# The last 20 destinations of a sampled-graph aggregation as one row of their own

## The chip, the core and the metric

The kernel runs on one core of one Trainium2 chip. The metric is the device time of one execution in microseconds (us). The engines are TensorE (PE for its matmuls, PEld for its weight loads), VectorE (DVE), ScalarE (ACT), GpSimd (POOL) and SyncE (SP); SP, ACT and POOL also issue DMA transfers.

## The reference

There are 12,500 nodes with 64 features and 800,000 edges with random source and destination. For each destination the features of its sources are summed, the sum is scaled by a given factor for each node, and two 64x64 products are added:

```python
N, deg, D = 12500, 64, 64
E = N * deg
nsum = _segment_sum(x[src], dst, N)
h_neigh = nsum * deg_inv[:, None]
return x @ w_self + h_neigh @ w_neigh
```

A destination has about 64 edges, so the last 20 destinations have about 1,280 of them.

## The kernel before, in words

**Buckets.** Destinations stand in 79 blocks of 160 (two halves of `HN` = 80), sources in `NB` = 98 blocks of 128. An edge belongs to the bucket (destination block, source block); there are `NBID` = 79 x 98 = 7742 buckets with about 104 edges each. The 79th block has only 20 destinations, since 12,500 = 78 x 160 + 20, so its 98 buckets hold about 13 edges each. An edge is one 32-bit key: destination block, source block, half, source within the block, destination within the half.

**Sorting.** `sort_edges` lays the 800,000 keys out as 128 runs of 6,250 and sorts each run on DVE. `find_rows` counts in every run how many keys lie below the first key of each of 256 rows. A row is a stretch of consecutive buckets: the first part has 128 rows of 37 buckets, the second 128 rows of 24 (`KPRS`). POOL gathers each row's piece out of each run (`gather_runs`), and DVE merges the 128 pieces of every row (`merge_runs`, L446).

**Finding buckets.** `find_and_gather` handles one bucket number k of all 128 rows at a time. `count_below` (L592 for the second part, on DVE) counts the keys below the middle of bucket k in a window of the merged row. The window must hold that place for each of the 128 rows, so the planning class `Windows` makes it as wide as the spread between the rows (5.5 standard deviations at either end). Four steps later (`LAG`) ACT turns the count into an address (L615) and POOL gathers 190 keys around it (L596). `decode_buckets` splits the keys: DVE (L633 to L638), ACT casts (L643, L647), POOL writes the sources to memory (L645), PE transposes (L653), ACT stores the destinations in `dlT` (L654). Keys outside the 64 slots of a half-bucket go through `leftovers`, and `rest` gathers their feature rows in groups of 128 (L811) and adds them with a matmul (L827).

**Summing.** `nodes` walks the buckets in tiles of 8. `one_hots` prepares 28 buckets at a time: SP loads their sources, copied to all partitions (L761), DVE compares them with the partition number (L763) and the destinations with a ramp (L766). For each bucket PE multiplies the 128 feature rows by the first one-hot (`ct`, L792), ACT or DVE copies a tile of eight out of PSUM (`xg`, L802 or L800; DVE takes part from tile 503 on), and two more matmuls add the bucket into the accumulators of its destinations (`acc`, L847). Six destination blocks make a group. At its end the accumulators are copied to `g` (L851 on ACT, L853 on DVE), and `finish` multiplies 480 destinations at a time by the weights (L911), scales them, adds the self term (L917, L918) and stores them (L919). The self terms are loaded by `load_own` (L895).

**Order.** From the sort on, every engine executes its instructions in the order in which this Python code issues them. The loop over `nodes` in `sums_and_merge` interleaves the rest: while tiles of the first part are summed, the second part is merged, then found (one step each second tile), then decoded (one step a tile), then its leftovers are handled. An engine that waits holds all that stands behind it in its queue. `finish` uses SP for its store where the self terms were loaded ahead, and POOL elsewhere.

The kernel also counts every key that it has placed; if the sum is not 800,000, a slow general path (`general`) computes the result instead.

Of the kernel before, what the change touches and what calls it, by code (L numbers as in the profile page):

```python
# [11 lines left out]
F32 = mybir.dt.float32  # L12
BF = mybir.dt.bfloat16
FH = mybir.dt.float16
I32 = mybir.dt.int32
U32 = mybir.dt.uint32
# [6 lines left out]
NB = 98  # L23
H = 64
HN = 80
NDB = -(-N // (2 * HN))
NBID = NDB * NB
FB = 120
NQ = -(-N // (4 * FB))
# [1 line left out]
PITCH1 = 6400  # L31
UPPER1 = 3500

KPRS = (37, 24)
ROWS = (128, 128)
BASE = (0, 128 * KPRS[0])
NCOL = 128 * sum(KPRS)
# [28 lines left out]
LAST = 20  # L66
LAG = 4
OCT = 6


def bid_base(b):
    b = np.asarray(b)
    v = 0x40000000 | (b // NB << 22) | (b % NB << 15)
    return np.where(b >= NBID, 0x7F000000, v).astype(np.uint32)


def bid_cum(mid=False):

    size = np.minimum(128, N - 128 * np.arange(NB))
    dsize = np.minimum(2 * HN, N - 2 * HN * np.arange(NDB))  # L80
    c = np.concatenate([[0], np.cumsum(np.outer(dsize, size))]) / float(N) ** 2
    if mid:
        c[:-1] += np.outer(np.minimum(HN, dsize), size).ravel() / float(N) ** 2
    return np.concatenate([c, np.ones(NCOL - NBID)])


class Windows:
# [56 lines left out]

def constants():
    thr = bid_base(np.concatenate([BASE[p] + np.arange(ROWS[p]) * KPRS[p] for p in range(2)]))
    act = np.array([on_act(c) for c in range(NC1)])
    t1 = np.where(act, -(thr - 1).view(np.float32), thr.view(np.float32))
    mul = np.where(act, -1.0, 2.0)
    add = np.array([(n if a else 0) + lo - 1 for (lo, n), a in zip(WIN.w1, act)])  # L150
    add[128:] -= UPPER1
    assert max(lo + 2 * n for lo, n in WIN.w1[:128]) + WIDE[0] <= SPLITS[1]
    assert min(lo for lo, _ in WIN.w1[128:]) > UPPER1
    c1 = np.zeros((128, 3, NC1), np.float32)
    c1[:, 0], c1[:, 1], c1[:, 2] = t1, mul, add
    out = {"c1": c1}
    for p in range(2):
        kpr = KPRS[p]
        b = BASE[p] + np.arange(128)[:, None] * kpr + np.arange(kpr)[None]
        v = bid_base(np.minimum(b, NBID))  # L160
        act = np.array([on_act2(p) for k in range(kpr)])
        first = np.array([lo + (n / 2 + 0.25 if a else 0) for (lo, n), a in zip(WIN.w2[p], act)])
        mid = v | np.uint32(1 << 14)
        c2 = out[f"c2_{p}"] = np.zeros((128, 6, kpr), np.float32)
        c2[:, 0] = v.view(np.float32)
        c2[:, 1] = mid.view(np.float32)
        c2[:, 2] = -(mid - 1).view(np.float32)
        c2[:, 3] = np.where(act, -0.5, 1.0)
        at = [home(p, k) for k in range(kpr)]
        c2[:, 4] = first + np.arange(128)[:, None] * np.array(PITCH2)[at] - np.where(np.array(at) == 1, UPPER2 + SIDE, 0)  # L170
        c2[0::2, 5, 0] = c2[1::2, 5, 1] = 1.0
    return out
# [79 lines left out]
class Kernel:  # L252
# [10 lines left out]
    def setup(self):  # L263
# [4 lines left out]
        self.idf = keep.tile([128, 128], F32, name="idf")  # L268
        make_identity(nc, self.idf)
        self.xh = keep.tile([128, NB, 2, D], FH, name="xh")  # L270
        self.cnt = keep.tile([128, sum(NCNT) + 3], F32, name="cnt")
        nc.gpsimd.memset(self.cnt, 0.0)
        self.deg = keep.tile([FB, 4 * NQ], F32, name="deg")
        self.wn = keep.tile([128, D], F32, name="wn")
# [414 lines left out]
    def leftovers(self, part, mps):  # L689
# [42 lines left out]
        self.left[part] = (place, src)  # L732
        yield 1

    def uses(self):


        out = []
        for o in range(0, NBID, OCT * NB):
            end = min(o + OCT * NB, NBID)  # L740
            here = []
            for p in range(2):
                for c in range(64):
                    lo = max(o, BASE[p] + c * 2 * KPRS[p])
                    hi = min(end, BASE[p] + (c + 1) * 2 * KPRS[p])
                    if hi > lo:
                        here.append([hi + 56, p, c, lo // NB, (hi - 1) // NB])
            at = end + 8
            for use in sorted(here)[::-1]:
                at = use[0] = min(use[0], at - 24)  # L750
            out += sorted(here)
        return out
# [16 lines left out]
    def nodes(self, pool, aps, mps):  # L769
# [61 lines left out]
        def sums(job):  # L831
# [17 lines left out]
            if last:  # L849
# [5 lines left out]
                for q in range(2):  # L855
                    if (2 * o + q) * 4 * FB < N:
                        late.append([b0 + 40 * (1 + 3 * q), self.finish(2 * o + q, g[:, q * 4 * FB:(q + 1) * 4 * FB],
                                                                        self.fin, mps, self.w2n, own)])
            return last

        tiles = []
# [3 lines left out]
        for t, (b0, cnt) in enumerate(tiles):  # L865
# [8 lines left out]
                else:  # L874
                    late[0][0] = b0 + 40
            if t == len(tiles) - 12:
                own = self.load_own(NQ - 1, self.fin)
            done.append(t)
            yield t
        for job in pend:  # L880
# [171 lines left out]
    def sums_and_merge(self, es, mps, aps, u1, other, l2, l2b, l2a, va, vp):  # L1052
# [17 lines left out]
        va.close()  # L1070

        self.fin = fin = es.enter_context(tc.tile_pool(name="fin", bufs=1, side="right"))
        find = decode = None
        self.left = {}
        self.picked, self.used = -9, 0
        left, left_at = self.leftovers(0, mps), 2
        t = 0
        for n in self.nodes(fin, aps, mps):
# [7 lines left out]
                    left_at = n + wait  # L1086
            if runs and n % 2:
                self.gather_runs(1, u1, [runs.pop(0)])
            if merge and n >= 8 and (n >= RESUME or steps < 2 * per):
                t += PACE  # L1090
                while merge and t > 0:
# [13 lines left out]
            elif find:  # L1105
                if n % 2 == 0 and self.picked < n - 1 and next(find, None) is None:
                    find = None
                    decode = self.decode_buckets(1, self.v, vp, mps)
            elif decode:
                if next(decode, None) is None:  # L1110
                    assert n < 128 * KPRS[0] // 8 - 12
# [31 lines left out]
```

## Time and profile before

| | |
|---|---|
| time, three runs | 1947.45 us median (1946.54 to 1955.99) |
| the profiled execution, its own time | 1940.29 us |
| its span, first to last instruction | 1938.5 us |
| busy: DVE, ACT, PE, POOL | 88%, 61%, 50%, 41% of the span |
| granted clock of TensorE, mean | 0.794 of full speed |

The summing loop fills the time from about 840 us to the end; PE is mostly idle before it. The stretches that the change touches all lie in this loop: 1291 to 1384 us (finding the second part), 1384 to 1426 us (decoding it), 1426 to 1500 us (its leftovers), and the end from 1900 us.

In a row of a timeline stand the start, the duration, the engine, the line, the operation, what it writes and reads, and in brackets how long the engine was idle before it and what ended that. A row of a stretch has busy time and count for each engine, the granted clock, the DMA share and GB/s. A row of waits has who waited for whom, the total in us, how often, and the longest.

### The profile page before, as it was taken

How to read it: one execution, taken by the hardware profiler on the slowest of the kernel's cores; microseconds unless marked ns; L12 is line 12 of the kernel's file. 1: busy time of each engine (PE TensorE's matmuls, PEld its weight loads, DVE VectorE, ACT ScalarE, POOL GpSimd, SP SyncE). 2: the span in 40 equal slices, each digit the busy share in tenths (PEclk: the TensorE clock that was granted, in tenths of full speed). 3: DMA queues.
4: the chain of work that ended last, by engine and by line, in shares of the span. 5: the costliest groups of instructions: out<-in, count | busy, mean ns of one | idle time of the engine just before them, and what ended most of it. 6: DMA issues, size and time to landing. Idle time of an engine off the chain costs nothing.

```text
span 1938.5 us, 55055 instructions
## 1 busy us (share of the span) xinstructions
PE 978.3 (50%) x23940; PEld 852.7 (44%) x23940; DVE 1707.2 (88%) x1729; ACT 1177.3 (61%) x1845; POOL 789.2 (41%) x904
## 2 busy tenths in 40 slices
PE   0043000000000000158888898886879998999896
PEld 0032000000000000047777777775768787887785
DVE  7999999995749997878799999999988889888884
ACT  7363007423510023448888898887868887888785
POOL 1000000498889984888423131325422233232231
PEclk9996555555555555579999999999989999999998
DMA  4332000011110012257677877887757888888873
GB/s 149 68 75 57 0 0 28 26 52 21 22 20 10 10 44 69 55 207 258 213 240 237 259 248 252 251 291 234 247 200 263 283 285 259 275 268 262 275 249 107
DMA packets 104053, 308.61 MB, mean 159 GB/s; under 512 B 51823, under 2 KB 59359, under 8 KB 103163
## 3 DMA queue, kind: packets, MB, share of 16 engines
q1 hardware_dynamic: 85963, 280.86, 40.9%
q0 software_dynamic: 17264, 22.07, 8.6%
q8 instruction: 189, 3.10, 0.6%
q10 hardware_dynamic: 576, 2.07, 0.3%
q14 instruction: 61, 0.50, 0.1%
HBM read 285.51 MB, written 19.44 MB: 157 GB/s over the span
## 4 chain that ended last, share of the span: by engine, by line
DVE 45%; PE 22%; POOL 15%; issue 10%; DMA 4%; ACT 3%; DVEq 0%; SPq 0%; ACTq 0%; POOLq 0%
DVE u L446 14%; PE ct L792 11%; POOL u L384 11%; PE acc L847 8%; DVE ohd L766 8%; DVE a L220 7%; DVE b L220 6%; DVE ohs L763 5%; POOL pad L297 3%; DVE junk L592 1%; DMA slb<-sl 1%; DVE u L406 1%; DMA lx<-xt,lsrc 1%; ACT xg L802 1%; DMA rd<-dst 1%
## 5 line engine op out<-in xcount | busy, mean ns | idle before, releaser
L802 ACT ACTIVATE xg<-ct 128x1024 f16<-128x1024 f32 (+1 forms) x909 | 864.2, 1034 | 171.0 <-PE ct L792 147.2
L792 PE MATMUL ct<-xh,ohs 128*128 128x128 f16 x7742 | 548.8, 224 | 63.8 <-DVE ohs L763 42.2
L792 PEld LDWEIGHTS <-ohs 128*128 128x128 f16 x7742 | 456.1, 100 | 104.9 <-issue 38.0
L384 POOL DMA_INDIRECT u<-d,ix x256 | 359.0, 1402 | 232.7 <-DVE ix L376 191.0
L847 PE MATMUL acc<-ohd,xg 64*128 64x80 f16 x15484 | 407.3, 200 | 66.0 <-issue 32.5
L446 DVE TENSOR_TENSOR u<-u 128x1456 f32<-128x1456 f32 (+46 forms) x292 | 393.7, 1377 | 21.6 <-ACT u L411 14.6
L847 PEld LDWEIGHTS <-xg 64*128 64x128 f16 x15484 | 323.5, 96 | 134.3 <-issue 62.2
L766 DVE TENSOR_TENSOR ohd<-iota,dlT 128x2240 f16<-128x2240 bf16 x277 | 365.4, 1319 | 0.0
L811 POOL DMA_INDIRECT lx<-xt,lsrc x140 | 234.4, 1675 | 286.1 <-PE acc L827 250.1
L763 DVE TENSOR_SCALAR ohs<-slb,pidx 128x3584 f16<-128x3584 bf16 x277 | 319.7, 1154 | 32.6 <-PE ct L792 23.9
L374 PE MATMUL stp<-idf,st 128*128 128x128 f32 x2 | 0.9, 447 | 368.0 <-DVE st L372 368.0
L919 POOL DMA_DIRECT2D out<-o x26 | 25.1, 964 | 375.1 <-DVE o L918 285.7
L220 DVE TENSOR_TENSOR a<-b 128x764 f32<-128x764 f32 (+39 forms) x104 | 171.6, 1693 | 3.9
L220 DVE TENSOR_TENSOR b<-a 128x764 f32<-128x764 f32 (+39 forms) x104 | 171.5, 1691 | 3.6
L374 PEld LDWEIGHTS stp<-idf,st 128*128 128x128 f32 x2 | 0.4, 183 | 368.4 <-issue 368.4
L653 PE MATMUL tr<-idb,l 128*128 128x128 bf16 x61 | 8.1, 271 | 284.1 <-ACT l L647 280.6
L800 DVE CAST xg<-ct 128x1024 f16<-128x1024 f32 x66 | 80.8, 1223 | 64.1 <-PE ct L792 63.8
L653 PEld LDWEIGHTS <-l 128*128 128x128 bf16 x61 | 5.0, 116 | 287.4 <-ACT l L647 283.2
L411 ACT ACTIVATE u<-u 128x30 f32<-128x30 f32 (+34 forms) x136 | 29.7, 265 | 152.5 <-DVE u L446 77.3
L596 POOL DMA_INDIRECT v<-d,ix x61 | 80.2, 1314 | 61.5 <-ACT ix L615 30.8
L222 ACT ACTIVATE b<-a 128x1 f32<-128x1 f32 (+21 forms) x52 | 18.1, 379 | 134.5 <-DVE a L220 129.4
L590 ACT ACTIVATE junk<-u,c 128x166 bf16<-128x166 f32 (+36 forms) x37 | 26.7, 723 | 119.1 <-DVE u L446 119.0
(136 smaller groups left out, 868.3 us busy)
## 6 DMA issues: line engine op xcount, KB each, us to landing
slb<-sl SPq DMA_DIRECT2D x277, 896.0 KB
u<-d,ix POOLq DMA_INDIRECT x256
xt<-xh SPq DMA_DIRECT2D x1, 3136.0 KB
fo<-own SPq DMA_DIRECT2D x26, 120.0 KB
out<-o POOLq DMA_DIRECT2D x26, 120.0 KB
own<-os SPq DMA_DIRECT2D x12, 256.0 KB
lx<-xt,lsrc POOLq DMA_INDIRECT x140
rd<-dst SPq DMA_DIRECT2D x4, 521.0 KB
```

The lines of the kernel that those rows point to most:

```text
L220: nc.vector.tensor_tensor(view(dst, lo + sh, [[st, g], [1, l]]), x, y, op=op)
L297: self.nc.gpsimd.memset(self.pad, 0.0)
L384: nc.gpsimd.indirect_dma_start(out=u[:nr, EDGE + p * w:EDGE + (p + 1) * w], out_offset=None, in_=src, in_offset=bass.IndirectOffsetOnAxis( ...
L446: nc.vector.tensor_tensor(view(dst, EDGE + o + out, d), view(src, EDGE + o + x, d), view(src, EDGE + o + x + gap, d), op=op)
L596: self.nc.gpsimd.indirect_dma_start(out=self.v[:, k].bitcast(F32), out_offset=None, in_=flat(self.d2[home(part, k)], 128 * PITCH2[home(par ...
L763: nc.vector.tensor_scalar(s.rearrange("p c s -> p (c s)"), b, self.pidx[:, :1], None, op0=OP.is_equal)
L766: nc.vector.tensor_tensor(d, self.iota[:, None].to_broadcast([128, 14, HN, 2]), ix, op=OP.is_equal)
L792: nc.tensor.matmul(ct[:, i * 128:(i + 1) * 128], cols[i][0], self.xh[:, (b0 + i) % NB].rearrange("p a f -> p (a f)"), start=True, stop=True)
L800: nc.vector.tensor_copy(xg[:, :cnt * 128], ct[:, :cnt * 128])
L802: nc.scalar.activation(xg[:, :cnt * 128], ct[:, :cnt * 128], AF.Copy)
L811: nc.gpsimd.indirect_dma_start(out=x, out_offset=None, in_=self.xt, in_offset=bass.IndirectOffsetOnAxis(ap=self.left[p][1][:, c:c + 1], ax ...
L847: nc.tensor.matmul(acc[h][:, db % OCT * HN:(db % OCT + 1) * HN], xg[r, i * 128:(i + 1) * 128], d[r], start=db % OCT == 0 and sb == 0, stop ...
```

## The change

The last 20 destinations get no buckets. There are 78 destination blocks and 7644 buckets, and rows of the second part hold 23 buckets. The buckets now fill the first 127 rows of that part, and the threshold of the 128th row is set to the first key of the 79th block (`TAIL`), so that this row collects the keys of the last 20 destinations and nothing else. After the merge a new generator, `tail`, reads 128 x 14 keys of that row, splits them, gathers the feature row of each key (14 indirect DMAs of 128 rows), makes a 128x20 one-hot for each 128 keys, adds them with 14 matmuls, and runs `finish` for the 20 destinations. It advances by one step each second tile, from the end of finding on. The self terms of the last two sets of 480 destinations, not those of the last 20, are now loaded ahead.

```diff
-NDB = -(-N // (2 * HN))
+NDB = N // (2 * HN)
-KPRS = (37, 24)
+KPRS = (37, 23)
+LEAST = 2 * HN * NDB
+LEND = 14
+TAIL = np.uint32(0x40000000 | NDB << 22)
...
-    return np.concatenate([c, np.ones(NCOL - NBID)])
+    return np.concatenate([c, np.full(NCOL - NBID, c[-1])])
...
+    thr[-1] = TAIL
...
+    def tail(self, mps):
+        nc = self.nc
+        pool = self.fin
+        n = LEND
+        k = pool.tile([128, n], I32, name="tk")
+        last = self.d2[2][127, SIDE:SIDE + 128 * n]
+        nc.gpsimd.dma_start(k.bitcast(F32), last.rearrange("(p n) -> p n", n=n))
+        yield
+        yield
...
+        nc.vector.tensor_scalar(s, k, 8, 0x3F80, op0=OP.logical_shift_right, op1=OP.bitwise_and)
+        nc.vector.tensor_scalar(t, k, 7, 0x7F, op0=OP.logical_shift_right, op1=OP.bitwise_and)
+        nc.vector.tensor_tensor(s, s, t, op=OP.bitwise_or)
+        yield
...
+        nc.vector.tensor_scalar(t, k, 21, 0xFE, op0=OP.logical_shift_right, op1=OP.bitwise_and)
+        nc.vector.tensor_scalar(z, t, float(2 * NDB), None, op0=OP.is_equal, op1=OP.add,
+                                accum_out=self.cnt[:, sum(NCNT) + 3:sum(NCNT) + 4])
+        nc.vector.tensor_scalar(q, k, 127, None, op0=OP.bitwise_and)
+        nc.vector.scalar_tensor_tensor(q, t, float(HN), q, op0=OP.mult, op1=OP.add)
+        nc.vector.tensor_scalar(t, k, 14, 1, op0=OP.logical_shift_right, op1=OP.bitwise_and)
+        nc.vector.scalar_tensor_tensor(z, t, float(HN), q, op0=OP.mult, op1=OP.add)
+        rows = pool.tile([128, n, 128], FH, name="tx")
+        for c in range(n):
+            yield
+            nc.gpsimd.indirect_dma_start(
+                out=rows[:, c], out_offset=None, in_=self.xt,
+                in_offset=bass.IndirectOffsetOnAxis(ap=s[:, c:c + 1].bitcast(U32), axis=0))
+        m = pool.tile([128, n, N - LEAST], FH, name="tm")
+        for c in range(n):
+            if c % 4 == 0:
+                yield
+            nc.vector.tensor_scalar(m[:, c], self.wide[:, :N - LEAST], z[:, c:c + 1], -float(LEAST),
+                                    op0=OP.subtract, op1=OP.is_equal)
+        yield
+        yield
+        yield
+        ps = mps.tile([128, N - LEAST], F32, name="tps", tag="ct", bufs=3)
+        for c in range(n):
+            nc.tensor.matmul(ps, rows[:, c], m[:, c], start=c == 0, stop=c == n - 1)
+        g = pool.tile([128, N - LEAST], F32, name="tg")
+        nc.scalar.activation(g, ps, AF.Copy)
+        yield
+        for _ in self.finish(NQ - 1, g, pool, mps, self.w2n):
+            yield
+            yield
...
-                                                                        self.fin, mps, self.w2n, own)])
+                                                                        self.fin, mps, self.w2n, own and own[q])])
...
-                own = self.load_own(NQ - 1, self.fin)
+                own = [self.load_own(NQ - 3 + q, self.fin) for q in range(2)]
...
+            if tail and n % 2:
+                next(tail, None)
...
+                    tail = self.tail(mps)
```

The lines of the changed file are numbered higher: L592 there is L599, L643 and L645 are L650 and L652, L811 is L868, L919 is L976.

The first place where the order differs is DVE's queue near the end of finding (the last four windows of 24 before, the last three of 23 now). Before:

```order
L766 TENSOR_TENSOR ohd<-iota,dlT 128x2240
L819 TENSOR_SCALAR ohl<-wide,lp_2467 128x160
L853 COPY g<-acc_13573 128x6x80
L592 TENSOR_SCALAR junk_15896,acc_1_14110<-u,c_1_68 128x2229
L763 TENSOR_SCALAR ohs<-slb,pidx 128x3584
L766 TENSOR_TENSOR ohd<-iota,dlT 128x2240
L592 TENSOR_SCALAR junk_15962,acc_1_14110<-u,c_1_68 128x2329
L763 TENSOR_SCALAR ohs<-slb,pidx 128x3584
L766 TENSOR_TENSOR ohd<-iota,dlT 128x2240
L592 TENSOR_SCALAR junk_16026,acc_1_14110<-u,c_1_68 128x2428
L592 TENSOR_SCALAR junk_16091,acc_1_14110<-u,c_1_68 128x2527
```

After:

```order
L823 TENSOR_TENSOR ohd<-iota,dlT 128x2240
L876 TENSOR_SCALAR ohl<-wide,lp_2467 128x160
L910 COPY g<-acc_13573 128x6x80
L599 TENSOR_SCALAR junk_15896,acc_1_14110<-u,c_1_68 128x549
L820 TENSOR_SCALAR ohs<-slb,pidx 128x3584
L823 TENSOR_TENSOR ohd<-iota,dlT 128x2240
L599 TENSOR_SCALAR junk_15962,acc_1_14110<-u,c_1_68 128x561
L820 TENSOR_SCALAR ohs<-slb,pidx 128x3584
L823 TENSOR_TENSOR ohd<-iota,dlT 128x2240
L599 TENSOR_SCALAR junk_16026,acc_1_14110<-u,c_1_68 128x573
```

The places stay the same, but the windows shrink: from 127 to 2527 keys wide (32,579 in sum) to 114 to 573 wide (9,197 in sum). Before, a row of the second part could hold buckets of the 79th block, with an eighth of the keys of the others, and the window of bucket k had to hold both; now all buckets are alike.

The second place is POOL's queue while the second part is decoded; `tk` are the keys of the last row, `tx` their feature rows, `sl` the sources of four decoded buckets, `lx` the feature rows of leftovers. Before:

```order
L811 DMA lx<-xt,lsrc_2469 128x128 x2
L645 DMA sl<-l_16701 128x512
L919 DMA out<-o 120x4x64
L645 DMA sl<-l_16836 128x512
L645 DMA sl<-l_16968 128x512
L811 DMA lx<-xt,lsrc_2469 128x128
L645 DMA sl<-l_17102 128x512
L645 DMA sl<-l_17232 128x512
```

After:

```order
L749 DMA tk<-d_2_66 128x14
L652 DMA sl<-l_16580 128x512
L868 DMA lx<-xt,lsrc_2469 128x128
L770 DMA tx<-xt,ts 128x128
L652 DMA sl<-l_16730 128x512
L976 DMA out<-o 120x4x64
L770 DMA tx<-xt,ts 128x128 x2
L652 DMA sl<-l_16867 128x512
L770 DMA tx<-xt,ts 128x128 x2
L652 DMA sl<-l_17001 128x512
L868 DMA lx<-xt,lsrc_2469 128x128
```

Two `tx` gathers now stand ahead of most of the `sl` writes. The 14 gathers are issued over 28 tiles, and the matmuls that read them are issued seven steps (14 tiles) after the last of them.

The third place is ACT's queue at the end of the loop. Before:

```order
L851 ACTIVATE g<-acc_29310 128x6x80
L802 ACTIVATE xg<-ct 128x1024 x9
L912 ACTIVATE o<-po 120x256
L802 ACTIVATE xg<-ct 128x1024
L802 ACTIVATE xg<-ct 128x256
L851 ACTIVATE g<-acc_31537 128x80
L912 ACTIVATE o<-po 120x256
L912 ACTIVATE o<-po 20x64
```

After:

```order
L859 ACTIVATE xg<-ct 128x1024 x12
L969 ACTIVATE o<-po 120x256
L859 ACTIVATE xg<-ct 128x1024 x42
L859 ACTIVATE xg<-ct 128x512
L908 ACTIVATE g<-acc_29388 128x6x80
L969 ACTIVATE o<-po 120x256 x2
```

The 13 tiles of the 79th block and their copy to `g` are gone; the two sets of 480 destinations of the last full group, which before were finished during and after those tiles, now come after the last `g` together.

More of the change, by code (lines that the diff above doesn't have):

```diff
@@ L146, in constants @@
     thr = bid_base(np.concatenate([BASE[p] + np.arange(ROWS[p]) * KPRS[p] for p in range(2)]))
+    assert thr[-1] == 0x7F000000 and thr[-2] < TAIL
+    thr[-1] = TAIL
     act = np.array([on_act(c) for c in range(NC1)])
@@ L270, in setup @@
         self.xh = keep.tile([128, NB, 2, D], FH, name="xh")
-        self.cnt = keep.tile([128, sum(NCNT) + 3], F32, name="cnt")
+        self.cnt = keep.tile([128, sum(NCNT) + 4], F32, name="cnt")
         nc.gpsimd.memset(self.cnt, 0.0)
@@ L733, in leftovers @@
         yield 1
+    def tail(self, mps):
[7 more added lines that the diff above has]
+        yield
+        t = pool.tile([128, n], I32, name="tt")
+        s = pool.tile([128, n], I32, name="ts")
+        nc.vector.tensor_scalar(s, k, 8, 0x3F80, op0=OP.logical_shift_right, op1=OP.bitwise_and)
+        nc.vector.tensor_scalar(t, k, 7, 0x7F, op0=OP.logical_shift_right, op1=OP.bitwise_and)
+        nc.vector.tensor_tensor(s, s, t, op=OP.bitwise_or)
+        yield
+        q = pool.tile([128, n], I32, name="tq")
+        z = pool.tile([128, n], F32, name="tz")
+        nc.vector.tensor_scalar(t, k, 21, 0xFE, op0=OP.logical_shift_right, op1=OP.bitwise_and)
[29 more added lines that the diff above has]
+            yield
@@ L1072, in sums_and_merge @@
         self.fin = fin = es.enter_context(tc.tile_pool(name="fin", bufs=1, side="right"))
-        find = decode = None
+        find = decode = tail = None
         self.left = {}
```

## The prediction

> **What bounds the kernel now.** I read the span first, then the stretches of the summing loop, then the waits and the chain in the stretches that the change touches. Columns: us, then busy time and count of PE, PEld, DVE, ACT, POOL, the clock, the DMA share, GB/s.
>
> ```profile
> span 1938.5 us, 55055 instructions
> ...
> 1000.00:1291.00 291.00, 251.36 (x6401) 218.63 (x6402) 290.50 (x265) 254.01 (x291) 72.74 (x38) 0.97 0.78 251
> 1291.00:1384.00 93.00, 73.15 (x1806) 64.38 (x1807) 90.25 (x106) 73.92 (x102) 46.00 (x32) 0.90 0.76 249
> 1384.00:1426.00 42.00, 33.37 (x851) 28.48 (x850) 40.75 (x68) 41.16 (x54) 20.72 (x17) 1.00 0.78 249
> 1426.00:1500.00 74.00, 62.50 (x1538) 55.58 (x1540) 62.89 (x94) 52.02 (x59) 12.51 (x9) 0.88 0.69 230
> ...
> 1500.00:1900.00 400.00, 361.42 (x9455) 317.51 (x9449) 343.45 (x371) 322.30 (x348) 115.57 (x78) 0.99 0.84 270
> ```
>
> The bound moves. From 1000 to 1291 us (merging) DVE is busy 290.5 of 291. In finding, 1291 to 1384, DVE is busy 90.25 of 93, while PE and ACT need 73 and 74. In decoding, 1384 to 1426, ACT is full (41.16 of 42) with DVE just behind (40.75). After 1500 PE leads with 361 of 400. The share of DVE over the whole span (88%) would hide this.
>
> What a bucket costs in each stretch follows from the count of its first matmul (PE busy and count, PEld, clock, DMA):
>
> ```profile
> 1000.00:1291.00 291.00, 148.91 (x2088) 122.28 (x2088) 0.97 0.78 251
> 1291.00:1384.00 93.00, 42.59 (x588) 35.62 (x589) 0.90 0.76 249
> ...
> 1500.00:1900.00 400.00, 210.25 (x3071) 175.16 (x3072) 0.99 0.84 270
> ```
>
> That is 0.139 us a bucket in merging, 0.158 in finding, 0.130 at the end (400 / 3071). Finding is the slow one, and the waits say why; the third row is of the stretch 1426 to 1500.
>
> ```profile
> PE acc L847 <- DVE g L853: 8.2, 1, 8.2
> PE ct L792 <- DVE ohs L763: 8.0, 4, 2.7
> ...
> PE lps L727 <- DVE lab L724: 9.3, 1, 9.3
> ```
>
> In finding PE stands 19.9 us (93 - 73.15), and 16.2 of them it waits for DVE: for one-hots, and once for the copy of a finished accumulator. On DVE's timeline that copy stands behind the counts:
>
> ```profile
> 1291.01 0.34 DVE L592 TENSOR_SCALAR_CACHE_REDUCE junk<-u,c 128x127 bf16<-128x127 f32 x1
> ...
> 1355.27 1.15 DVE L763 TENSOR_SCALAR ohs<-slb,pidx 128x3584 f16<-128x3584 bf16 x1
> 1356.34 1.32 DVE L766 TENSOR_TENSOR ohd<-iota,dlT 128x2240 f16<-128x2240 bf16 x1
> 1357.57 0.25 DVE L819 TENSOR_SCALAR ohl<-wide,lp 128x160 f16<-128x160 f16 x1
> 1357.74 0.65 DVE L853 COPY g<-acc 128x480 f32<-128x480 f32 x1
> ...
> 1370.69 2.85 DVE L592 TENSOR_SCALAR_CACHE_REDUCE junk<-u,c 128x2527 bf16<-128x2527 f32 x1
> ```
>
> In the chain that ended last, cut to 1291 to 1440 us, these counts are the largest part:
>
> ```profile
> by line: DVE junk L592 18.6%; DVE ohd L766 16.6%; issue 14.3%; DVE ohs L763 11.9%; DMA slb<-sl 6.5%; PE ct L792 6.5%; ACT xg L802 6.4%; DMA v<-d,ix 3.6%; PE acc L847 3.1%; DVE top L687 2.4%; ACT l L647 2.1%; DVE ohl L819 1.5%; DVE u L672 1.
> ```
>
> A count grows from 0.34 us at 127 keys to 2.85 at 2527: 1.046 ns a key, plus 0.21 us.
>
> **The change part by part.**
>
> *Narrower windows.* The 24 windows hold 32,579 keys, the 23 new ones 9,197 (the widths are in DVE's queue). DVE is relieved of 23,382 x 1.046 ns = 24.5 us in a stretch in which it is the bound. PE and ACT cannot go below 73 to 74 us there, so at most 19 us can be had. If just the two waits for DVE vanish, the stretch takes 76.8 us; at the rate of the end, 588 x 0.130 = 76.6; at the rate of merging, 588 x 0.139 = 82. DMA moved 0.76 x 93 = 71 us of full work there; at the 0.84 of the end it needs 84. I take 80: **-13 us**, between -9 (84) and -16.4 (76.6).
>
> *Decoding.* ACT is its bound, and the change takes from ACT only a quarter of one of six groups. On DVE come nine small operations of the tail, each below the 0.19 us of a row four times as wide (the first below), so at most 1.7 us; the last group saves about a quarter of its split. PE's 9.3 us wait for DVE at the leftovers (L727) thus stays about as it is: DVE has little lead at the start of decoding, since a one-hot buffer comes free only when PE is through with it. **0**, between -3 (it keeps some lead) and +3.
>
> *The tail's other work.* POOL gets 14 gathers and one load in decoding and after it; rows of the operations nearest to what is added:
>
> ```profile
> L704 DVE TENSOR_SCALAR ls<-ltop 128x64 int32<-128x64 int32 x1 | 0.2, 191 | 0.0
> ...
> L827 PEld LDWEIGHTS <-lx x280: 95/98/152, 869.1 to 1923.9; 128*128 128x128 f16 x140
> L827 PE MATMUL acc<-ohl,lx x280: 199/210/341, 869.1 to 1924.0; 128*128 128x80 f16 x77, 128*128 128x160 f16 x63
> L811 POOL DMA_INDIRECT lx<-xt,lsrc x140: 938/1616/4315, 861.3 to 1904.4; - x140
> ```
>
> At the median the gathers cost POOL 14 x 1.62 = 23 us. With the 20.72 us that it already works in decoding and about 1 for the load of the keys this is 45 us for a stretch of 42. What hangs on POOL there are the `sl` writes: ACT's cast reuses a buffer two groups later, 8 tiles, or 8 x 42 / 34 = 9.9 us (272 buckets are 34 tiles). So POOL may run up to 52 us before ACT waits: the gathers cost nothing, and if that cover is gone they cost us for us. The 14 matmuls come 14 tiles after the last gather, so they find their rows landed. On PE they cost 14 x 0.1 (weights, the matmul beside them) to 14 x 0.3 (one after the other), 1.4 to 4.2 us; the 14 one-hots on DVE at most 14 x 0.19 = 2.7, in a stretch where DVE idles 11 of 74; the copies on ACT and the finish of 20 rows below 1 together. In that stretch PE is the fuller engine. **+2**, between 0 and +5.
>
> [...]
>
> *The end.* 98 buckets go, 13 tiles: 98 x 0.130 = 12.8. From one copy of the accumulators to the next it was 14.9 us (1910.82 to 1925.68 below); **-13**, between -12 and -15.
>
> ```profile
> 1910.82 0.57 ACT L851 ACTIVATE g<-acc 128x480 f32<-128x480 f32 x1 [0.42 <-PE acc L847]
> 1912.48 0.66 DVE L853 COPY g<-acc 128x480 f32<-128x480 f32 x1
> 1921.17 1.00 PE L911 MATMUL po<-w2n,g 128*120 128x64 f32 x8
> 1924.12 0.54 PE L847 MATMUL acc<-ohd,xg 64*128 64x80 f16 x20
> 1925.68 0.24 ACT L851 ACTIVATE g<-acc 128x80 f32<-128x80 f32 x1 [1.59 <-PE po L911]
> 1925.81 0.38 ACT L912 ACTIVATE o<-po 120x256 f32<-120x256 f32 x1
> 1925.89 0.42 DVE L917 TENSOR_TENSOR o<-o,deg 120x256 f32<-120x256 f32 x1
> 1926.34 0.43 DVE L918 TENSOR_TENSOR o<-o,fo 120x256 f32<-120x256 f32 x1
> 1930.03 0.43 DVE L918 TENSOR_TENSOR o<-o,fo 120x256 f32<-120x256 f32 x1 [2.93 <-DMA fo<-own]
> 1930.37 0.21 ACT L912 ACTIVATE o<-po 20x64 f32<-20x64 f32 x1 [4.18 <-DMA out<-o]
> 1930.75 0.81 POOL L919 DMA_DIRECT2D out<-o  x1 [2.85 <-DVE o L918]
> ```
>
> *After the last sum.* Before, 6.1 us passed from the last matmul (1924.66) to POOL's last large store (1930.75), with a wait for self terms and one for an output buffer. Now all that follows the last matmul is the copy of 480 columns (0.66), two sets of matmuls (1.0 each), ACT's 0.38, DVE's 0.42 and 0.43, and handovers, about 0.3: 4.2 us. The self terms were loaded ahead, no output buffer is in use, and SP issues the stores. **-2.5**, of which 1.9 are this difference and the rest POOL's issue; between 0 (SP's store lands later) and -5 (POOL's closing work, now free of a late store, drops out of the 7 us that follow).
>
> Elsewhere nothing changes: merging keeps its lengths, and the leftovers their 140 gathers.
>
> **Sum.** -13 + 0 + 2 - 13 - 2.5 = -26.5. The profiled execution took 1940.3, so 1913.8; the median of the runs, 1947.45, lies 7.2 above it, so I predict **1921**.
>
> **Rivals.** *Finding is held by others* (ACT at 74, DMA, gathers of 190 keys on POOL every second tile): it takes 89 and not 80. For: DMA at 0.76 beside it; against: PE waits for DVE 16.2 us, for nothing else so long. 1930.
>
> *DVE's relief carries on*: finding falls to 76.6, and DVE enters decoding so far ahead that the 9.3 us wait shrinks to 1: -3.4 - 8.3, 1909. For: DVE works almost without a pause from 1291 to the wait. Against: the one-hot buffers bound its lead.
>
> *POOL starves decoding* (slower than before): in its queue `sl` writes stand behind two `tx` gathers each, ACT's cast waits for the buffer, and ACT holds every eviction. The loss is 20.7 + 1 + 14c - 51.9 for c us a gather. It eats all the gain from c = 4.05 on; at the slowest row, 4.3, it is 30 us: 1951. For: POOL would be full; against: the median is 1.62.
>
> *The change doesn't do what it says*: a key of the last row is missed, the count is off, and the general path runs. It has 250 x 25 x 3 indirect transfers, at 0.94 us at least 17,600 us. Against: 1,792 places for about 1,280 keys.
>
> **How the numbers follow.** Forecast 0.68, finding held 0.12, relief carried on 0.13, POOL starved 0.05 (half of it slower by over 0.5%), general path 0.02. A measurement of this kernel can tell about 0.5% (9.7 us) from no change. The first three cases are all faster by more than that, with a little taken off for two terms failing together: faster 0.92, same 0.04, slower 0.04. The terms' bounds taken together reach from -39 to -13; the range 1907 to 1934 holds these, and leaves out the starved and the general case.
>
> **What will show it.** Finding: the stretch from the first to the last L599 with the waits for DVE gone and PE above 88% busy; L599 in all 14 to 16 us. Decoding: ACT still full, no wait of ACT for `sl`, `tx` gathers near 1.6 us. Leftovers: the wait at L734 still 6 to 12 us. The 14 `tps` matmuls without a wait of PE for `tx`. The end: two `po` sets right after the last `g`, stores on SP. I am wrong if finding stays above 85 us, if ACT or PE waits for POOL's DMAs, or if the loop's last 98 buckets were worth less than 11 us.

## The result, and the profile after

| | before | after |
|---|---|---|
| median, same chip | 1948.68 us (1946.54 to 1955.99) | 1918.35 us (1908.14 to 1924.20) |
| profiled execution, its own time | 1940.29 us | 1924.20 us |
| its span | 1938.5 us | 1922.5 us |

The ratio is 0.9838 (95% interval 0.9805 to 0.9870): 30 us less, 25 to 38 by the interval. The forecast was 26.5 us less, 1921. Compared twice more, on two chips, the pair gave 0.985 (0.9812 to 0.9887) and 0.9853 (0.9830 to 0.9876). The profiled execution of the changed kernel was the slowest of its four, while that of the kernel before lay below its median, so the two traces differ by 16 us only; they are compared stretch by stretch.

First, from the page of the profile of the changed kernel, its span and its busy times.

```profile
span 1922.5 us, 54475 instructions
...
PE 966.5 (50%) x23659; PEld 837.4 (44%) x23659; DVE 1675.0 (87%) x1740; ACT 1170.4 (61%) x1833; POOL 805.8 (42%) x917
```

Then the stretches of the loop: finding, decoding with the leftovers, and the long rest. The columns are those of the prediction's stretches.

```profile
1293.00:1366.00 73.00, 67.29 (x1644) 57.56 (x1638) 64.65 (x100) 66.92 (x93) 43.28 (x30) 0.96 0.90 307
1366.00:1423.00 57.00, 39.35 (x928) 33.47 (x923) 50.39 (x114) 45.74 (x59) 36.91 (x31) 0.93 0.64 208
...
1445.00:1913.00 468.00, 419.50 (x10820) 367.31 (x10818) 385.97 (x419) 369.42 (x401) 133.57 (x89) 0.98 0.79 253
```

And the first matmuls of the buckets (L849) alone, in finding: PE's and PEld's time and count, clock, DMA share, GB/s.

```profile
1293.00:1366.00 73.00, 39.22 (x540) 32.12 (x540) 0.96 0.90 307
```

In finding, DVE was busy 90 of 93 us before; now it has 64.65 of 73, and PE leads with 67.29, ACT just behind with 66.92. A bucket costs 73 / 540 = 0.135 us there, against 0.158. The counts and the waits say why; first the changed kernel's counts (duration in ns: least, median, greatest).

```profile
L599 DVE TENSOR_SCALAR_CACHE_REDUCE junk<-u,c x23: 324/647/798, 1293.7 to 1354.6; 128x114 bf16<-128x114 f32 x1, 128x180 bf16<-128x180 f32 x1, 128x220 bf16<-128x220 f32 x1, 128x251 bf16<-128x251 f32 x1
```

Then the waits of finding (first row) and of decoding (the others).

```profile
DVE ohs L820 <- PE ct L849: 5.1, 8, 1.2
...
PE lps L734 <- DVE lab L731: 8.4, 1, 8.4
...
DVE ts L754 <- DMA tk<-d: 3.8, 1, 3.8
```

No count takes over 0.8 us, where the longest took 2.85. The direction of the wait has turned: DVE now waits for PE (5.1 us) to free a one-hot buffer, where PE waited for DVE 16.2 us. PE's wait at the leftovers is still there (8.4, before 9.3). New is a wait of DVE in decoding: the first operation on the keys of the last row (`ts`, L754) stands until their load has landed. On the timeline POOL issues that load (L749) at 1369.70, and DVE goes on at 1375.82, 6.1 us after the issue began:

```profile
1369.70 1.25 POOL L749 DMA_DIRECT2D tk<-d  x1
1370.75 1.32 DVE L823 TENSOR_TENSOR ohd<-iota,dlT 128x2240 f16<-128x2240 bf16 x1
...
1375.82 0.17 DVE L754 TENSOR_SCALAR ts<-tk 128x14 int32<-128x14 int32 x1 [3.75 <-DMA tk<-d]
```

The rest of the tail is cheap. These are its gathers, its one-hots and its matmuls, from the views of each:

```profile
L770 POOL DMA_INDIRECT tx<-xt,ts x14: 940/978/1997, 1380.9 to 1419.3; - x14
...
L777 DVE TENSOR_SCALAR tm<-wide,tz x14: 213/216/228, 1427.0 to 1435.0; 128x20 f16<-128x20 f16 x14
...
L784 PE MATMUL tps<-tm,tx x14: 171/171/185, 1439.1 to 1439.4; 128*128 128x20 f16 x14
```

The gathers take 0.98 us in the middle, not the 1.62 of the leftovers' gathers, and the 14 matmuls, one behind the other, about half a microsecond together.

The end of the timeline after:

```profile
1912.30 0.81 PE L904 MATMUL acc<-ohd,xg 64*128 64x80 f16 x24
1913.14 0.57 ACT L908 ACTIVATE g<-acc 128x480 f32<-128x480 f32 x1 [0.41 <-PE acc L904]
1913.18 0.66 DVE L910 COPY g<-acc 128x480 f32<-128x480 f32 x1 [7.42 <-PE acc L904]
1913.98 1.86 PE L968 MATMUL po<-w2n,g 128*120 128x64 f32 x16 [0.87 <-DVE g L910]
...
1916.37 1.19 SPq L976 DMA_DIRECT2D out<-o  x2
1916.76 0.42 DVE L975 TENSOR_TENSOR o<-o,fo 120x256 f32<-120x256 f32 x1
```

Both sets of 480 destinations are finished together behind the last copy, with no wait for self terms or an output buffer, and SP issues the stores. From the last matmul (1913.11) to the end it is 9.4 us, before 13.9. From the last full group's copy to `g` (1910.82 before, 1913.14 after) to the end it is 27.7 us before and 9.4 after: 18.3 us less, for the 98 buckets and for what follows them.

### The profile page after: what moved, and what is told of

Same layout as the page of the kernel before. It is cut to its first block, busy times and chain, and to the rows that moved or that the text cites. A ratio compares the mean times of both kernels' runs of the same rounds, so it can differ in the third digit from the quotient of the medians.

```text
span 1922.5 us, 54475 instructions
## 1 busy us (share of the span) xinstructions
PE 966.5 (50%) x23659; PEld 837.4 (44%) x23659; DVE 1675.0 (87%) x1740; ACT 1170.4 (61%) x1833; POOL 805.8 (42%) x917
## 4 chain that ended last, share of the span: by engine, by line
DVE 47%; PE 21%; POOL 13%; issue 11%; DMA 4%; ACT 3%; DVEq 0%; SPq 0%; ACTq 0%; POOLq 0%
DVE u L453 15%; PE ct L849 12%; POOL u L391 10%; PE acc L904 8%; DVE ohd L823 7%; DVE a L227 7%; DVE b L227 7%; DVE ohs L820 5%; POOL pad L304 2%; ACT xg L859 2%; DMA slb<-sl 1%; DVE u L413 1%; ACT junk L597 1%; DMA rd<-dst 1%; PE po L968 1%
## 5 line engine op out<-in xcount | busy, mean ns | idle before, releaser
L849 PE MATMUL ct<-xh,ohs 128*128 128x128 f16 x7644 | 543.1, 223 | 74.6 <-DVE ohs L820 43.2
L849 PEld LDWEIGHTS <-ohs 128*128 128x128 f16 x7644 | 448.6, 100 | 119.0 <-issue 51.1
L904 PE MATMUL acc<-ohd,xg 64*128 64x80 f16 x15288 | 401.8, 199 | 55.0 <-issue 31.6
L904 PEld LDWEIGHTS <-xg 64*128 64x128 f16 x15288 | 317.6, 96 | 123.9 <-issue 53.0
L823 DVE TENSOR_TENSOR ohd<-iota,dlT 128x2240 f16<-128x2240 bf16 x273 | 359.5, 1317 | 0.0
L820 DVE TENSOR_SCALAR ohs<-slb,pidx 128x3584 f16<-128x3584 bf16 x273 | 313.9, 1150 | 44.8 <-PE ct L849 33.3
L868 POOL DMA_INDIRECT lx<-xt,lsrc x140 | 237.6, 1697 | 265.8 <-PE acc L884 232.1
L976 POOL DMA_DIRECT2D out<-o x25 | 23.2, 929 | 362.4 <-DVE o L975 297.7
```

Of the source, the lines that this page charges most:

```text
L820: nc.vector.tensor_scalar(s.rearrange("p c s -> p (c s)"), b, self.pidx[:, :1], None, op0=OP.is_equal)
L823: nc.vector.tensor_tensor(d, self.iota[:, None].to_broadcast([128, 14, HN, 2]), ix, op=OP.is_equal)
L849: nc.tensor.matmul(ct[:, i * 128:(i + 1) * 128], cols[i][0], self.xh[:, (b0 + i) % NB].rearrange("p a f -> p (a f)"), start=True, stop=True)
L868: nc.gpsimd.indirect_dma_start(out=x, out_offset=None, in_=self.xt, in_offset=bass.IndirectOffsetOnAxis(ap=self.left[p][1][:, c:c + 1], ax ...
L904: nc.tensor.matmul(acc[h][:, db % OCT * HN:(db % OCT + 1) * HN], xg[r, i * 128:(i + 1) * 128], d[r], start=db % OCT == 0 and sb == 0, stop ...
```

## The experiments

Ratios are to the kernel before on the same chip, with their 95% intervals. The twelve timings of this section stood on three chips, four on each. The changed kernel itself was timed again beside the three variants of the first chip and the three of the last; the four of the middle chip are set against the kernel before alone.

### The changed kernel again, as the yardstick

> The changed kernel again, as the base that the other kernels of this study are held against, with a second trace. Theory: the ratio to the kernel before is 0.984 as before, 1917 us. In the first trace of the change the six last groups of 588 buckets took 468 us against 456 before; if this is scatter between executions, the second trace shows them at 456 to 462; the rival, that the change itself slows the last stretch, says 466 or more.

1920.43 us, 0.985 (0.9812 to 0.9887), a gain of 29 us, near the first. But the six last groups of 588 buckets took 469.1 us in this trace, where scatter was to show 456 to 462 and the rival 466 or more. Whether the change slows that stretch thus needs the other traces; it is taken up at the end of the next section.

### The windows as wide as before

```diff
+BEFORE = ((40, 127), (48, 249), (56, 365), (65, 476), ..., (253, 2329), (265, 2428))
...
+            if part:
+                ws = list(BEFORE)
```

The 23 windows hold 30,052 keys again instead of 9,197, at the places where they stood before. (The counts' scratch tile is shared by both parts, for room.)

> The change with the windows of the second part as wide as before (30,052 keys in 23 windows, where the change has 9,197). Nothing is left out. Theory (DVE bounds finding, 1.046 ns a key): DVE has 21.8 us more to do while it finds, finding takes 16 to 20 us longer than in the change, the copy of the accumulators stands behind counts again, and the whole is 13 to 20 us slower than the change. Rival (finding was held by ACT or DMA): at most 6 us slower.

1936.32 us, 0.9939 (0.9908 to 0.9970): 17 us of the gain are gone, by the difference of the ratios. The stretch of finding is 88 us long again, with DVE busy in 84.86 of it:

```profile
1290.00:1378.00 88.00, 69.62 (x1705) 60.88 (x1704) 84.86 (x100) 70.34 (x96) 41.55 (x31) 0.88 0.75 253
```

and the wait of PE for the copy of the accumulator is back (L915 here is L910 of the changed kernel, L739 its L734):

```profile
PE lps L739 <- DVE lab L736: 10.3, 1, 10.3
...
PE acc L909 <- DVE g L915: 7.8, 1, 7.8
```

So the relief of DVE in finding is worth about 17 us (the two intervals together leave room for 8 to 27), where -13 was predicted with a bound of -16.4. The traces, which are free of the scatter elsewhere, give 11 to 15 us for the stretch from the first count to the first split, a little less than the 16 to 20 expected: 87.8 us here, 72.5, 77.0 and 72.6 in three executions of the change.

### No tail

```diff
-                    tail = self.tail(mps)
```

The last 20 destinations are not computed at all, and the count of placed keys no longer decides on the general path.

> The change without the generator that sums the last 20 destinations: their 20 rows of the output are left out, and the count of placed keys, which lacks them, no longer decides over the general path. Theory: the tail costs more than the 2 us of the prediction, because DVE stands 3.8 us for the late load of its keys at the start of decoding and is behind from there to the leftovers; without it the kernel is 5 to 8 us faster than the change, and the wait of PE at the leftovers falls from 8.4 us to 3 to 6. Rival (the tail is hidden but for its own matmuls): 1 to 3 us faster. Second rival (POOL's gathers hold the decoding): above 8 us.

1914.35 us, 0.9809 (0.9755 to 0.9862). That is 6 us below the change by the medians and 8 by the ratios, but the intervals overlap widely. The traces don't find these microseconds where the tail's work stands. Finding and decoding up to the leftovers' matmul take 73.8 + 55.2 = 129.0 us without the tail:

```profile
1293.90:1367.70 73.80, 62.62 (x1622) 54.84 (x1616) 64.53 (x102) 66.73 (x92) 38.82 (x31) 0.98 0.89 300
1367.70:1422.90 55.20, 38.87 (x958) 33.62 (x952) 47.81 (x101) 45.48 (x58) 17.97 (x16) 0.94 0.62 211
```

With it they take 128.6 (72.5 + 56.1), 131.8 and 128.5 in three executions. POOL has 18 us of work in decoding without the tail and 37 with it, and the stretch is as long. PE's wait at the leftovers is 6.5 us, where 3 to 6 was expected. So the tail costs nothing that the stretch shows and 8 us by the ratios, whose intervals together leave room for -5 to +21. The runs don't fix it better; the prediction's 0 to 5 lies within, and neither the theory nor its rivals are told apart.

### The load of the last row's keys issued early

```diff
                         find = self.find_and_gather(1, range(KPRS[1]), LAG)
+                        first = self.tail(mps)
+                        next(first)
...
-                    tail = self.tail(mps)
+                    tail = first
```

The load `tk` is issued when finding begins, not when it has ended; the rest of the tail stays where it was.

> The change with the load of the last row's keys issued when finding begins, some 60 tiles earlier, and all else of the tail where it was. Theory: DVE's wait of 3.8 us for this load goes, DVE reaches the leftovers that much earlier, PE waits there 4 to 5 us and not 8.4, and the kernel is 3 to 4 us faster than the change. Rival (ACT is the bound of decoding, so DVE's wait was covered): within 1.5 us of the change.

1915.37 us, 0.9829 (0.9789 to 0.9869): 5 us below the change, too little to tell. It was timed again with the change beside it:

> The changed kernel once more, beside the three variants below, since differences of 3 to 8 us can't be read across chips. Theory: ratio to the kernel before 0.985; six last groups of 588 buckets 460 to 470 us.

> The early load of the last row's keys again. Theory: 3 to 6 us faster than the change on the same chip. Rival (the first difference was scatter): within 2 us.

The change took 1912.63 us, 0.9853 (0.9830 to 0.9876); with the early load 1903.29, 0.9789 (0.9771 to 0.9807). The intervals lie apart: **9 to 12 us faster** by the medians and the ratios, more than the 3 to 6 expected, and the best version of this study. (The trace of the change had 456.3 us for its six last groups, below the 460 to 470 expected.) Finding and decoding, up to the leftovers' matmul, take 121.1 us here, in the change beside it 128.5; in the first pair it was 124.0 against 131.8. PE's wait at the leftovers fell from 10.3 us to 7.3 and 6.6, not to the 4 to 5 expected. These are all the waits of DVE in that stretch, first of the change, from 1295 to 1424:

```profile
DVE ohs L820 <- PE ct L849: 5.3, 6, 2.4
DVE ts L754 <- DMA tk<-d: 4.7, 1, 4.7
DVE ohs L820 <- DMA slb<-sl: 2.8, 1, 2.8
```

and with the early load, from 1292 to 1413:

```profile
DVE ohs L820 <- PE ct L849: 5.3, 6, 2.4
DVE ohs L820 <- DMA slb<-sl: 0.3, 1, 0.3
```

with the two parts of that stretch, finding and decoding:

```profile
1291.70:1361.80 70.10, 62.11 (x1632) 53.88 (x1631) 64.14 (x101) 66.23 (x93) 43.72 (x33) 1.00 0.90 317
1361.80:1412.80 51.00, 36.34 (x919) 31.27 (x919) 49.64 (x110) 45.01 (x58) 38.18 (x30) 0.97 0.69 226
```

The waits fall by 4.7 + 2.5 = 7.2 us and the stretch by 7.4. The first part was the aim: DVE is busy 49.64 of 51.00 us in decoding, so it is the bound there. The second, a wait for a load of sources (`slb`) at the beginning of finding, was not foreseen. With the early load POOL waits 7.0 us for the merged rows to reach memory before it can read the last of them, and its first gathers come later; that they no longer delay the load of `slb` is argued, not shown.

That the stretch is shorter because these waits are gone is argued too, and two other traces speak against it as the whole cause. Without the tail there is no wait for `tk`, and with every gather twice (below) it is 1.4 us, yet the stretch takes 129.0 and 129.2 us. In both DVE stands for PE instead; first the kernel without the tail (1290 to 1440), then the one with the gathers twice (1290 to 1445):

```profile
DVE ohs L820 <- PE ct L849: 11.6, 7, 2.5
```

```profile
DVE ohs L824 <- PE ct L853: 9.9, 7, 2.7
```

In the two traces above this was 5.3 us. PE itself stands 13.2 us without a named cause in the stretch of the kernel without the tail, 7.6 in that of the change and 5.3 with the early load. Whether the early load shortens these pauses, or whether they differ by scatter, is open.

### The sums without the 79th block, in the kernel before

```diff
+SUMS = 78 * NB
...
-        for o in range(0, NBID, OCT * NB):
-            end = min(o + OCT * NB, NBID)
+        for o in range(0, SUMS, OCT * NB):
+            end = min(o + OCT * NB, SUMS)
...
-                own = self.load_own(NQ - 1, self.fin)
+                own = [self.load_own(NQ - 3 + q, self.fin) for q in range(2)]
```

This is the kernel before, with 24 buckets a row and its wide windows. It leaves out the sums of the 79th block, so the last 20 destinations get no result, and loads the self terms of the last two sets ahead. It does the end of the change alone.

> The kernel before without the sums of the 79th block: its 98 buckets are sorted, found and decoded, but not summed, and the last 20 rows of the output are left out; the self terms of the last two sets are loaded ahead, as in the change. Theory: this is the end alone. The loop loses 13 us (98 buckets at 0.130), and what follows the last matmul falls from 13.9 us to the 9.4 to 10.0 that the traces of the change show: 17 us faster than before in all, 1932. Rival (the pauses of PE and the last group's drain swallow part of it): below 10 us faster.

1927.0 us against 1945.85, 0.9896 (0.9875 to 0.9917): 20 us less by the ratio (16 to 24), where 17 was expected. The end looks as in the change; from the last copy to `g` to the end of the span (1933.6) it is 9.2 us:

```profile
1924.40 0.57 ACT L852 ACTIVATE g<-acc 128x480 f32<-128x480 f32 x1 [0.41 <-PE acc L848]
...
1925.24 1.89 PE L912 MATMUL po<-w2n,g 128*120 128x64 f32 x16 [0.87 <-DVE g L854]
...
1927.62 1.20 SPq L920 DMA_DIRECT2D out<-o  x2
```

The end is worth 18.3 us by the traces and 20 on the chip; -15.5 was predicted for it (-13 and -2.5).

### The leftovers' matmul ten tiles later

```diff
+        if part:
+            yield 10
```

ahead of the matmul `lps` (L734), where PE waits 8.4 us for DVE's `lab`.

> The change with the matmul of the second part's leftovers (L734), for which PE waits 8 to 10 us, issued 10 tiles later than its operands are computed on DVE. Nothing is left out. Theory: DVE is that far behind PE only at this place and has 15 to 25% idle time behind it, so PE goes on summing with the one-hots that it has, the wait vanishes, and the kernel is 5 to 9 us faster than the change. Rival (PE would wait for one-hots instead, since DVE is just as late with them): within 2 us of the change.

1918.79 us, 0.9868 (0.9837 to 0.9898). The wait is gone from the trace, and the 5 to 9 us that were expected did not come: on the other chips the change had 0.985 and 0.9853. That PE's wait costs nothing because DVE, which is busy 88% of that stretch, goes on working meanwhile is argued.

> The change with both: the early load of the last row's keys and the leftovers' matmul 10 tiles later. Theory: the two take away the same lag in part, so less than their sum: 7 to 11 us faster than the change. Rival (both only move the same wait): as the better of the two alone, 5 us faster than the change.

> The early load and the leftovers' matmul 10 tiles later, again. Theory, after the first try with the later matmul alone gave no clear gain: the matmul's wait is PE time that the loop then spends waiting elsewhere, so as the early load alone within 3 us. Rival (the wait was worth its 8 us): 6 us or more faster than the early load alone.

Both edits together, the early load and the late matmul, took 1915.73 us, 0.9830 (0.9810 to 0.9851), and beside the change again 1911.25, 0.9814 (0.9791 to 0.9837). The early load alone was at 0.9789 there, 8 us lower by the medians where 3 at most was expected, though the intervals overlap: the late matmul adds nothing to it. It also means that only one of the three kernels with the early load on that chip (the third is the last of this section) is clearly faster than the change beside it. The 9 to 12 us belong to that one program; they are no price of a load that could be added to others.

### Every gather of the tail twice

```diff
+        spare = pool.tile([128, n, 128], FH, name="ty")
...
+            nc.gpsimd.indirect_dma_start(
+                out=spare[:, c], out_offset=None, in_=self.xt,
+                in_offset=bass.IndirectOffsetOnAxis(ap=s[:, c:c + 1].bitcast(U32), axis=0))
```

> The change with every gather of the tail issued twice (the second result is not used): 14 more indirect transfers, some 20 us of POOL's time, in the same 28 tiles. By the prediction's sum (20.7 + 1 + 28 x 1.62 - 52 = 15) ACT would wait for POOL's writes and the kernel be 15 us slower than the change, and so the same for gathers of twice the price. Rival (POOL has more cover than that sum gave, since it is busy only 37 of 57 us between the first split and the leftovers' matmul in the change's trace): at most 4 us slower.

1923.79 us, 0.9882 (0.9857 to 0.9906), some 6 us above the change by the ratios on other chips, at the edge of what can be told: between the 15 of the theory and the 4 of the rival. The gathers and POOL in the stretch of decoding:

```profile
L774 POOL DMA_INDIRECT ty<-xt,ts x14: 943/964/1852, 1381.5 to 1436.9; - x14
...
1369.00:1425.00 56.00, 40.37 (x951) 34.49 (x952) 51.16 (x118) 46.42 (x60) 40.90 (x33) 0.94 0.61 208
```

With 28 gathers POOL is busy 40.90 of 56 us; 20 of them fall ahead of the leftovers' matmul, where the change has its 14, and the others run on to 1437. Finding and decoding last as long as with 14 (75.8 + 53.4 = 129.2), and ACT has no wait for an `sl` write there. So POOL has room for six gathers more in this stretch, and nothing in it is held up by them.

### The tail behind the decoding

```diff
-                        self.check(fin, mps)
+                        tail = first
...
+                        first = self.tail(mps)
+                        next(first)
```

The keys are loaded early as above, but all else of the tail starts only when the second part's leftovers are through; the count of placed keys is summed up after it.

> The early load, and all further steps of the tail begun only when the second part's leftovers are through, so that decoding has neither its 14 gathers nor its nine small operations on DVE; the test of the count of keys is moved behind the tail's count. Theory (what the tail cost in decoding was the late load, and nearly nothing else): within 3 us of the early load alone, 3 to 8 us faster than the change. Rival (the gathers and operations delay decoding): 4 us or more faster than the early load alone.

1916.1 us, 0.9863 (0.9837 to 0.9890): no better than the change, and 13 us behind the early load alone. Both the theory and its rival missed. Finding and decoding are as short as with the early load alone (70.0 + 50.5 us, there 121.1). These two waits are new, from 1415 to 1480:

```profile
POOL tx L771 <- DVE ts L756: 12.2, 1, 12.2
...
PE fps L988 <- DVE one L986: 3.8, 1, 3.8
```

Of these the 3.8 us hold PE. But the two traces don't show where 13 us go: their executions differ by 6 us only (1909.26 and 1915.46), the stretch from the leftovers' matmul to the last one took 484.0 us with the early load alone and 485.0 here, and 7.3 us of difference lie ahead of the first count (at 1291.7 and 1299.0), where the two programs do the same. The loss is open.

## Why the prediction was right, and what was mis-sized in it

The forecast of 1921 us, with -26.5, meets 1918.35 and -30; the chance of 0.92 was on the right side. The terms, with their measure:

| term | predicted | by the traces | on the chip |
|---|---|---|---|
| narrower windows | -13 (-9 to -16.4) | -13.9 (588 buckets at 72.5 / 540 us) | -17 (-8 to -27) |
| decoding | 0 (-3 to +3) | +3.6 | in the tail's |
| the tail's other work | +2 (0 to +5) | not told from scatter | +8 (-5 to +21) |
| 98 buckets and what follows the last sum | -15.5 (-12 to -20) | -18.3 | -20 (-16 to -24) |

*Narrower windows.* The step was right in kind and close in size. DVE was the bound, it lost 24.7 us of counting (39.11 before, 14.44 now), and PE and ACT set the next bound: PE is busy 92% of the stretch (above 88% was said), the counts came out where they were expected (14 to 16), and the waits for DVE's copy are gone. The rate of 0.134 us a bucket lies between the two taken for it, 0.130 and 0.139. That finding is *held by others* at 89 us fell: its buckets cost 78.9 us. That DMA at 0.76 would hold it fell too: in the shorter stretch DMA went to 0.90. What the chip adds, 17 rather than 14 us, is within the intervals.

*Decoding.* Zero was given, on the ground that ACT is the bound there and that nine small operations cost DVE little. The first half of that failed. The stretch that was read ended at 1426, where PE's wait for DVE begins; up to the leftovers' matmul ACT stays at 41.16 us and DVE is the full one, in the kernel before:

```profile
1384.00:1433.00 49.00, 33.37 (x851) 28.48 (x850) 47.51 (x99) 41.16 (x54) 20.72 (x17) 0.96 0.75 242
```

In the change it is 50.39 of 57 for DVE and 45.74 for ACT, so the sign "ACT still full" did not come. The stretch has 16 buckets more than before (288 against 272, by the count of the first matmuls); at the old rate of 49.6 / 272 these are 52.5 us, and it took 56.1. The nine operations took the 1.7 us that were said, but the first of them waits 3.75 us for a load issued a few tiles earlier. The prediction counted the load as 1 us of POOL and gave no price to its landing. The size of this wait fits the 3.6 us; that it is their cause is not shown, since the stretch is as long in the two traces where the wait is gone or 1.4 us.

*DVE's relief carries on* fell: with finding as short as it is, PE still waits 8.4 us at the leftovers, and taking that wait away altogether brought nothing. The reason given, that the one-hot buffers bound DVE's lead, is seen in finding, where DVE waits 5.1 us for PE to free one.

*POOL starves decoding* fell. The gathers cost 978 ns in the middle; together they took 17.7 us, and by the prediction's own formula 20.7 + 1 + 17.7 = 39.4, well below the 51.9 us from which ACT would wait; ACT has no wait for the `sl` writes. Twenty gathers in place of 14 did not lengthen the stretch either. Beside a DVE that was busy 50.39 of 57 us each gather took 0.94 to 2.0 us (with every gather twice, one of the 28 took 3.06). The term took 1.62 from the leftovers' gathers, which was too much but on the safe side.

*The end.* Both terms were a little small. The last full group's matmuls end at 1910.81 in the kernel before (its copy starts at 1910.82) and the last matmul of all at 1924.66, so the 98 buckets took 13.8 us there, where -13 was taken. The 14.9 us between the two copies hold another 1.0 us behind the last matmul, which the next term counts. The larger miss is what follows the last matmul: it fell by 4.5 us, from 13.9 to 9.4, where 2.5 was taken (to 10.0 and 9.6 in two other executions of the change). Up to the end of DVE's last operation (1931.08 before, 1917.18 after) it fell by 2.3 us, close to the 1.9 of the sum. From there to the end of the span it fell by another 2.1, from 7.4 to 5.3 us, where 0.6 was taken: this closing part is the term that was mis-sized, inside its bound of -5. What shortens it, no run separates.

*The sum.* By the traces decoding lost 3.6 us where nothing was taken, and the end gained 2.8 more than taken. These two cancelled, which is luck. On the chip -20 at the end, -17 in finding and 0 to +8 for the tail with decoding give -29 to -37, against -29 to -32 in the three comparisons; the intervals in the table are too wide to say whether the gains and the tail are both larger than taken.

*What the single traces can't tell.* In the profiled execution of the change the rest of the loop, from the leftovers' matmul to the last one, took 490.8 us, as long as before (491.2) with 66 buckets less in it. In two other executions of the same kernel it took 490.5 and 477.3. The six full groups of 588 buckets took 457.8 us before and 468.1, 469.1 and 456.3 in the three executions of the change, with the same instructions but for the tail's last few. That the change itself slows them is contradicted by its third trace, and by the kernel before without the sums of its 79th block, where they took 467.2. So ±7 us of a single trace's span is scatter in that stretch, more than most of the terms; the stretches of finding and decoding repeat within 3.3 us in the change.

## What to carry to other kernels

Read the gain of a change from the waits of the stretch that it touches, and cap it by the busy time of the next engine there: that gave the term of finding within a microsecond by the traces, and within its interval on the chip. To find the bound, read a stretch up to the event that ends it, here the leftovers' matmul, and not up to where the wait for it begins. An operation added to an engine that is the bound can cost its wait besides its duration (here 3.75 us beside 0.17): ask when its input was asked for. For the end of a program price also what lies behind the last operation, up to the end of the span (here 7.4 us before and 5.3 after). A wait that is gone from a trace is not yet a gain, since the engine may stand for another one instead (here DVE for PE, 11.6 and 9.9 us in place of 5.3): look for a second kernel without it. And before believing a gain of a few microseconds in one trace, look at the scatter of a stretch that nobody touched (here ±7 us).

## What the runs showed of the hardware that was not expected

**PE pauses that nothing in the program explains.** In the long last stretch PE stands many times for 0.7 to 3 us without a wait for any engine. The rows of the kernel before (1453 to 1909 us), released by "issue":

```profile
PE acc L847 <- issue: 20.7, 22, 2.6
```

and of the change (1423 to 1913 us):

```profile
PE acc L904 <- issue: 22.3, 20, 2.4
...
PE ct L849 <- issue: 12.5, 8, 3.0
```

Beside them runs a DMA queue of instructions; here 60 us of the kernel before, 1500 to 1560, packets and MB:

```profile
q8 instruction: 12, 0.20, 1.2%
```

That is a packet of about 16 KB (0.20 MB / 12) each 5 us. In the change's last 468 us there are 84 of them, and PE and PEld execute 10,820 + 10,818 = 21,638 instructions, 258 for each packet, beside some 900 of DVE, ACT and POOL together; so the packets are most likely PE's own instructions, an estimate from these counts. Of the 26 pauses of PE above 0.7 us in that stretch, 38.7 us in all, 23 end 1.2 to 1.6 us after the end of such a packet, where a moment picked at random would do so one time in 14. (For five of the 26 the profile names an engine as well.) In the kernel before it is 17 of 19 (31.0 us). So 23 of the 84 packets have such a pause behind them, in the kernel before 17 of 85. That PE waits for its next instructions there is a guess from this coincidence in time and not shown: no kernel was made with fewer instructions on PE, and why a pause follows some packets and not others is open. The pauses alone don't make the scatter of ±7 us: in the execution of the change whose six groups took 456.3 us they sum to 38.1, nearly as much as the 38.7 in the one with 468.1.

**A small load is slow to arrive.** 128 x 14 keys, 7 KB, issued by POOL at 1369.70, let DVE go on at 1375.82. In the six executions that issue it behind finding, DVE stood 1.0 to 5.7 us for it; in the five that issue it when finding begins, DVE had no wait for it. No run loads more or fewer keys, so what part of the 6.1 us hangs on the size is not shown.
